# A pinned prologue for an attention and GLU kernel: one written order for four engines

## The chip, the cores and the metric

One core of a Trainium2 chip. The core's engines run side by side, each with an instruction stream of its own: TensorE (PE, matrix products), VectorE (DVE), ScalarE (ACT), GpSimd (POOL) and SyncE (SP, which issues the DMAs here). Matrix products land in PSUM, eight banks of 128 x 512 fp32; all else lives in SBUF. The metric is the device time of one launch in microseconds, the median of several runs.

## The reference

One transformer block with adaptive layer norm, on 2048 rows of 512: attention with 32 query heads of width 16 that share one key and one value head, then a gated feed-forward network of width 1792. Cut to what matters:

```python
mod = (silu(c) @ w_mod).reshape(1, 6, 1, 512)
sa, ca, ga, sb, cb, gb = (mod[:, i] for i in range(6))
h = layernorm(x) * (1 + ca) + sa
q, k, v = h @ wq, h @ wk, h @ wv          # q in 32 heads of 16; k and v one head of 16
p = softmax(q k^T * 16 ** -0.5)           # over 2048 keys
x = x + ga * ((p v) @ wo)
h = layernorm(x) * (1 + cb) + sb
out = x + gb * ((sigmoid(h @ w_gate) * (h @ w_up)) @ w_down)
```

Inputs and outputs are fp32. Most products run in fp16 with each operand split into a high and a low half, so that one product of full precision is three products (`passes`).

## The kernel before

The 2048 rows are four blocks of 512 (`b`). The kernel has three parts.

**Prologue.** Per block: the statistics and the normalization of layer norm (`row_norm`, line 253, called by `ln1_norm`), transposes to put the 512 features on partitions (`ln1_tr`, four chunks `k`), the evacuation that applies scale and shift and splits into high and low fp16 (`ln1_ev` with `split_evac`, line 276: high on ACT, the full fp32 part on ACT or DVE, and the difference on POOL or DVE), and the key and value products (`kv_block`, which writes the keys `kp`). The modulation vectors come from `mod_part`, `mod_cols` and `mod_rows`: four narrow fp32 products (`pmod`), a copy on ACT (`mod`), a product that sums the four parts (`pcol` or `prow`), and a last copy. Two query groups (a group is 128 query columns, four pairs of heads, of one block) are made here; each goes to DRAM (`qD`) and comes back in another layout (`qp`, `load_q`).

Before a score can be exponentiated its row's maximum over all keys is needed. So each *unit* (512 queries of four heads; 32 units in all, eight per block) has 64 score products `sa` with a maximum on DVE each (`a_tile`), then `max_end` and `max_rows`, which put the maxima as extra rows into `qp`, where the second score product `st` subtracts them. The prologue ends with the first `A0 = 76` of these maxima. In unit 0 they go query tile by query tile, so that a first tile's rows (`max_rows`) are ready early; `parts` then gives unit 0's `st` and `c` products as quarters of 128 columns that follow the query tiles.

The prologue's steps stand in the order of a short `PLAN`, but nothing is pinned there: `Ordered` keeps the order of PE, DVE and ACT only when `pinned` is filled, which happens at its end. Until then a scheduler reorders all engines by its own model. All banks of PSUM but one are one pool (`bank`); `cbank` is the accumulator.

**Main loop.** 32 units of 16 steps, PE, DVE and ACT in the written order. Each step has four `st` products with an exponential each (ACT), four `sa` products with a maximum each (DVE) for the units ahead, and the product with the values into `c` (`pv`, two steps behind). In block 0 the query groups that the prologue did not make run beside the steps, two groups as a couple over 17 steps (`light`, `early`); from block 1 on the feed-forward network of the block before does. At the end of a unit `unit_end` copies the accumulator (`cs`, DVE) and starts the next unit's. POOL splits the weights (`weight_jobs`).

**Tail.** The feed-forward network of the last block, not pinned.

Nearly all instructions of PE, DVE and ACT in the main loop are recorded at line 116, that of `Ordered`, so they are told apart by their tiles.

Of the kernel before, what the change touches and what calls it, by code (L numbers as in the profile page):

```python
# [16 lines left out]
P = 128  # L17
S = 2048
D = 512
H = 32  # L20
# [15 lines left out]
PLAN = 'n1 x2 l0 k0 x3 t1 l3 e1 w0 l1 n2 w3 k1 w1 q00 n3 q01 t2 t3 e2 e3 l2 m a1 k2 a2 k3 a4 w2 a8 p z3 a12 z4 a16 z2 a18 z5'  # L36

E32 = [(0, 1), (1, 1), (2, 0), (3, 3), (3, 1)]
ELO = [(0, 3), (0, 1), (3, 1), (3, 2), (2, 1), (3, 0), (1, 1)]

# [26 lines left out]
def adaln_mqa_glu_kernel(  # L67
# [24 lines left out]
    pc = ctx.enter_context(tc.tile_pool(name="pc", bufs=1, space=PSUM))  # L92
    psum = {}
    psum["ctx"] = ExitStack()
    psum["b"] = psum["ctx"].enter_context(tc.tile_pool(name="ps", bufs=1, space=PSUM))
# [4 lines left out]
    def bank(name):  # L100
        return psum["b"].tile([P, 512], F32, tag="b", name=name, bufs=psum.get("n", 7))

    def sbank(name):
        return psum["s"].tile([P, 512], F32, tag=name, name=name, bufs=SBANKS[name]) if "s" in psum else bank(name)

    def cbank(name):
        return pc.tile([P, 512], F32, tag="c", name=name, bufs=1)
# [10 lines left out]
    pinned = []  # L118
    pe, dve, act = Ordered(nc.tensor), Ordered(nc.vector), Ordered(nc.scalar)

# [78 lines left out]
    load_x(0)  # L199
    load_mod(1)  # L200
    load_mod(0)
# [17 lines left out]
    def mod_part(i):  # L219
        p_ = bank("pmod")  # L220
        for k in range(NDC):
            pe.matmul(p_[32 * k:32 * (k + 1)], cbc[:, k, :], wmods[i][:, k, :], start=True, stop=True)  # L222
        t_ = t32("mod")
        act.activation(t_, p_, AF.Identity)
        return t_

    def mod_cols(i, mul, add, name, t_=None):
        res = cp.tile([P, NDC], F32, name=name)
        t_ = mod_part(i) if t_ is None else t_
        p_ = bank("pcol")  # L230
        for m in range(NDC):
            pe.matmul(p_[:, m:m + 1], t_[:, m * P:(m + 1) * P], sel[:, 0:1], start=True, stop=True)
        dve.tensor_scalar(res, p_[:, :NDC], add, mul, op0=ALU.add, op1=ALU.mult)
        return res

    def mod_rows(i, scale, name):
        g_ = cp.tile([P, D], F32, name=name)
        t_ = mod_part(i)
        p_ = bank("prow")
        pe.matmul(p_, sel, t_, start=True, stop=True)  # L240
        act.activation(g_, p_, AF.Identity, scale=scale)
        return g_
# [33 lines left out]
    def split_evac(src, k, sc, sh, hi, lo, e32=None, elo=None):  # L276
        h32 = t32("h32")
        if pinned:
            act.activation(h32, src, AF.Identity, scale=sc[:, k:k + 1], bias=sh[:, k:k + 1])
            pool.tensor_scalar(hi, h32, 1.0, 0.0, op0=ALU.mult, op1=ALU.add)  # L280
            pool.tensor_tensor(lo, h32, hi, op=ALU.subtract)
            return
        act.activation(hi, src, AF.Identity, scale=sc[:, k:k + 1], bias=sh[:, k:k + 1])  # L283
        if e32 is None:
            act.activation(h32, src, AF.Identity, scale=sc[:, k:k + 1], bias=sh[:, k:k + 1])
        else:
            e32.tensor_scalar(h32, src, sc[:, k:k + 1], sh[:, k:k + 1], op0=ALU.mult, op1=ALU.add)
        (elo or pool).tensor_tensor(lo, h32, hi, op=ALU.subtract)


    kbias = cp.tile([P, 1], F32, name="kbias")
    pool.memset(kbias, 0.0)
    for j in (32, 96):
        pool.memset(kbias[j:j + 32], -SM)
        pool.memset(kbias[j:j + 16], 0.0)
# [6 lines left out]
    for t_, s_ in zip(wkr, (wkvh, wkvl)):  # L302
        dve.memset(t_, 0.0)
        for j in (0, 16, 32, 64, 80, 96):
            dve.tensor_copy(t_[:, :, j:j + DH], s_[:, 0])
# [9 lines left out]
    def split_wq(o):  # L315
        cols = slice(o * P, (o + 1) * P)
        w_, hi, lo = wqs.pop(o), wdh[:, :NDC, cols], wdl[:, :NDC, cols]
        act.activation(hi, w_, AF.Identity, scale=SW)
        dve.scalar_tensor_tensor(lo, w_, SW, hi, op0=ALU.mult, op1=ALU.subtract)
# [11 lines left out]
    pts = {}  # L331

    def ln1_norm(b):
        row_norm(xs(b), xs(b))

    def ln1_tr(b, k):
        pts[b, k] = pt = cbank("pt") if k % 4 == 1 else bank("pt")
        for t in range(4):
            pe.transpose(pt[:, t * P:(t + 1) * P], xs(b)[t][:, k * P:(k + 1) * P], ident)

    def ln1_ev(b, k):
        if b not in h1:
            h1[b] = [], []
        hh, hl = h1[b]
        hh.append(t16(f"h1h{k}"))
        hl.append(t16(f"h1l{k}"))
        split_evac(pts.pop((b, k)), k, sc1, sh1, hh[k], hl[k],
                   dve if (b, k) in E32 else None, dve if (b, k) in ELO else None)

    def ln1_block(b):  # L350
        for k in range(NDC):
            if (b, k) not in pts:
                ln1_tr(b, k)
        for k in range(NDC):
            ln1_ev(b, k)
# [4 lines left out]
    def kv_block(b):  # L360
        hh, hl = h1[b]
        pk = bank("pk")
        pv_ = bank("pv")
        n = 0
        for k in range(NDC):
            for w_, h_ in passes(wkr[0], wkr[1], hh[k], hl[k]):
                pe.matmul(pk, w_[:, k, :], h_, start=(n == 0), stop=(n == 3 * NDC - 1))
                n += 1
        for t in range(4):
            n = 0  # L370
            for k in range(NDC):
                for h_, w_ in passes(hh[k], hl[k], wkvh, wkvl):
# [3 lines left out]
        kb = kp[:, b * QB:(b + 1) * QB]  # L376
        act.activation(kb, pk, AF.Identity, scale=1.0 / (SH * SW), bias=kbias)
        for j in (32, 96):
            dve.scalar_tensor_tensor(kb[j:j + DH], pk[j:j + DH, :], 1.0 / (SH * SW), kb[j:j + DH],
                                     op0=ALU.mult, op1=ALU.subtract)  # L380
        dve.tensor_scalar(V[:, b * 4:(b + 1) * 4, 0:DH],
                          pv_[:, :4 * DH].rearrange("p (t d) -> p t d", t=4),
# [4 lines left out]
    def q_group(b, o):  # L387
# [5 lines left out]
        def end(pq, second):  # L393
# [3 lines left out]
            if second:  # L397
                dve.tensor_scalar(q32, pq, 1.0 / (SH * SW), None, op0=ALU.mult)
            else:
                act.activation(q32, pq, AF.Identity, scale=1.0 / (SH * SW))  # L400
            if pinned:
                pool.tensor_scalar(q2[:, 0], q32, 1.0, 0.0, op0=ALU.mult, op1=ALU.add)
            else:
                act.activation(q2[:, 0], pq, AF.Identity, scale=1.0 / (SH * SW))
            pool.tensor_tensor(q2[:, 1], q32, q2[:, 0], op=ALU.subtract)
            sp.dma_start(qD[:, o * P:(o + 1) * P, b * QB:(b + 1) * QB].rearrange("h p q -> p h q"), q2)

        return Group("q", 12, "pq", term, end)

# [11 lines left out]
    def load_q(b, o):  # L421
        qp = wp.tile([P, 4, QB], F16, tag="qp", name="qp", bufs=2)
        for j in (32, 96):
            pool.memset(qp[j:j + 32], 0.0)  # L424
# [18 lines left out]
    def a_tile(i, n):  # L443
        qp, pr0 = get_q(i)
        if i not in mxs:
            mxs[i] = wp.tile([P, 4, 4, 4], F32, tag="mx", name="mx", bufs=2)
        h = n % 4
        kc, qt = (n // 4 % 4, n // 16) if i == 0 else (n // 16, n // 4 % 4)
        j, pr = heads[h]
        sa = sbank("sa")  # L450
        pe.matmul(sa, qp[64 * j:64 * j + 64, pr0 + pr, qt * P:(qt + 1) * P],  # L451
                  kp[64 * j:64 * j + 64, kc * 512:(kc + 1) * 512], start=True, stop=True)
        dve.tensor_reduce(mxs[i][:, 2 * j + pr, qt, kc:kc + 1], sa, axis=AX.X, op=ALU.max)  # L453
        if i == 0 and n % 16 == 15:
            pend.append((i, n // 16, n // 16 + 1))
        elif i > 0 and n == 63:
            pend.append((i, 0, 4))

# [9 lines left out]
    def max_rows(i, t0, t1, m16):  # L468
# [6 lines left out]
        if pinned:  # L475
# [14 lines left out]
    def parts(i, t):  # L490
        if i == 0:
            return [(4 * (t % 4) + n, slice(n * P, (n + 1) * P), slice(t // 4 * P, (t // 4 + 1) * P)) for n in range(4)]
        return [(t, slice(0, QB), slice(0, QB))]

    def st_tile(i, t, pr, j):
# [5 lines left out]
        for kb, cols, qs in parts(i, t):  # L501
            pe.matmul(s_[:, cols], kp[64 * j:64 * j + 64, kb * P:(kb + 1) * P],
                      qp[64 * j:64 * j + 64, pr0 + pr, qs], start=True, stop=True)
# [5 lines left out]
    def pv(i, t, half=None):  # L509
        if t == 0 and half != 1:  # L510
            Cs[i] = cbank("c")
        ps = parts(i, t)
        if half is not None:
            if i == 0:
                ps = ps[2 * half:2 * half + 2]
            else:
                cut = slice(half * QB // 2, (half + 1) * QB // 2)
                ps = [(t, cut, cut)]
        for kb, cols, qs in ps:
            for hh in range(4):  # L520
                pe.matmul(Cs[i][32 * hh:32 * hh + 32, qs], V[:, kb, :], Ps[i, t, hh][:, cols],
                          start=(kb == 0 and (i == 0 or half != 1)), stop=(kb == NKB - 1 and (i == 0 or half != 0)))
# [7 lines left out]
    def unit_end(i):  # L530
# [3 lines left out]
        if pinned:  # L534
# [109 lines left out]
    def ffn_groups(b):  # L644
# [6 lines left out]
        def wo_group(t):  # L651
# [5 lines left out]
            def end(po, second):  # L657
# [3 lines left out]
                if second:  # L661
                    act.activation(t1, po, AF.Identity)
                    pool.tensor_tensor(t1, t1, mods2['ga'], op=ALU.mult)
# [137 lines left out]
    for tok in PLAN.split():  # L801
# [3 lines left out]
        elif f_ == "t":  # L805
            for k in range(NDC):
                ln1_tr(args[0], k)
# [222 lines left out]
```

## Time and profile before

| | |
|---|---|
| median of 3 runs | 1740.53 us (1739.78 to 1742.03) |
| span of the profiled execution | 1738.4 us; the page gives no other time for it |
| busy share of the span | PE 97%, DVE 83%, ACT 71%, POOL 35% |
| the largest groups | exponentials on ACT 1139.2 us, maxima on DVE 1241.2 us |
| prologue, to the first `st` product | 114.9 us |
| block 0, from there to the copy of its eighth unit | to 456.6 us |
| tail, from the last unit's copy | from 1592.4 us |

The page gives busy time per engine, the granted clock of TensorE in 40 slices, the chain of waits that ended last, and groups of instructions with their mean time and the idle time before them. A busy PE is not PE at its peak, since products overlap.

### The profile page before, as it was taken

How to read it: one execution, taken by the hardware profiler on the slowest of the kernel's cores; microseconds unless marked ns; L12 is line 12 of the kernel's file. 1: busy time of each engine (PE TensorE's matmuls, PEld its weight loads, DVE VectorE, ACT ScalarE, POOL GpSimd, SP SyncE). 2: the span in 40 equal slices, each digit the busy share in tenths (PEclk: the TensorE clock that was granted, in tenths of full speed). 3: DMA queues.
4: the chain of work that ended last, by engine and by line, in shares of the span. 5: the costliest groups of instructions: out<-in, count | busy, mean ns of one | idle time of the engine just before them, and what ended most of it. 6: DMA issues, size and time to landing. Idle time of an engine off the chain costs nothing.

```text
span 1738.4 us, 35892 instructions
## 1 busy us (share of the span) xinstructions
PE 1691.9 (97%) x14467; PEld 591.1 (34%) x14467; DVE 1443.2 (83%) x2407; ACT 1226.3 (71%) x2231; POOL 605.1 (35%) x715
## 2 busy tenths in 40 slices
PE   5889999999999999999999999999999999999998
PEld 3335333333233333333333333333333333333443
DVE  8889999999998988888899898988898888841311
ACT  3338888888878777777778777777778777774100
POOL 4131445454443332332245232233255141231433
PEclk9769999999999999999999999999999999999999
DMA  7111223231100110111111110011101010011211
GB/s 262 40 47 31 95 85 106 89 110 63 51 23 26 47 49 12 33 38 41 32 41 33 33 50 20 26 47 47 36 17 57 28 57 5 30 50 55 75 60 49
DMA packets 66238, 90.94 MB, mean 52 GB/s; under 512 B 14752, under 2 KB 41376, under 8 KB 66072
## 3 DMA queue, kind: packets, MB, share of 16 engines
q1 hardware_dynamic: 66072, 88.66, 15.6%
q8 instruction: 113, 1.85, 0.4%
q14 instruction: 53, 0.43, 0.1%
HBM read 67.68 MB, written 16.22 MB: 48 GB/s over the span
## 4 chain that ended last, share of the span: by engine, by line
PE 86%; DVE 7%; ACT 2%; POOL 1%; issue 1%; DMA 1%; SPq 0%; POOLq 0%; DVEq 0%; ACTq 0%
PE c L116 27%; PE st L116 20%; PE pgu L116 12%; PE sa L116 8%; PE pd L116 5%; PE pgu L139 4%; DVE mx L116 3%; PE pd L139 2%; PE pq L116 2%; PE po L116 2%; ACT P L116 2%; PE sa L451 1%; DVE mx L453 1%; PE pmod L222 1%; PE pt L116 1%
## 5 line engine op out<-in xcount | busy, mean ns | idle before, releaser
L116 ACT ACTIVATE P<-st 128x512 f32<-128x512 f32 x2048 | 1139.2, 595 | 283.7 <-PE sa L116 250.0
L116 DVE TENSOR_REDUCE mx<-sa 128x1 f32<-128x512 f32 x1972 | 1241.2, 684 | 113.6 <-PE sa L116 108.3
L116 PE MATMUL st<-qp,kp 64*128 64x512 f16 (+1 forms) x2240 | 746.8, 362 | 7.1 <-DVE mx L453 2.4
L116 PE MATMUL sa<-kp,qp 64*128 64x512 f16 x1972 | 725.3, 382 | 0.5 <-DVE mx L116 0.5
L116 PE MATMUL c<-P,V 128*32 128x512 f32 (+2 forms) x5552 | 577.6, 492 | 2.9 <-DVE cs L116 2.9
L116 PEld LDWEIGHTS <-kp 64*128 64x128 f16 x2240 | 187.8, 94 | 500.1 <-issue 407.2
L116 PE MATMUL pgu<-h2h,gw 64*128 64x512 f16 x1344 | 242.6, 376 | 0.0
L116 PEld LDWEIGHTS <-qp 64*128 64x128 f16 x1972 | 181.8, 93 | 137.0 <-issue 51.9
L116 PEld LDWEIGHTS c<-P,V 128*32 128x32 f32 x5552 | 111.5, 108 | 192.1 <-issue 177.3
L727 POOL TENSOR_SCALAR th<-th 128x512 f32<-128x512 f32 x42 | 26.0, 619 | 335.8 <-ACT th L116 325.8
L116 PE MATMUL pgu<-h2l,gw 64*128 64x512 f16 x672 | 132.3, 376 | 0.0
L116 PEld LDWEIGHTS <-gw 64*128 64x128 f16 x2016 | 99.6, 94 | 80.7 <-issue 3.1
L424 POOL MEMSET qp<- 32x2048 f16 x32 | 57.6, 1798 | 49.3 <-PE st L116 41.6
L139 PE MATMUL pgu<-h2h,gw 128*128 128x512 f16 x224 | 66.8, 379 | 0.5 <-ACT h2h L283 0.5
L733 POOL TENSOR_TENSOR gl<-th,gh 128x512 f16<-128x512 f32 x56 | 64.8, 1157 | 4.7
L478 POOL TENSOR_SCALAR mh<-m 16x128 f16<-16x128 f32 (+1 forms) x34 | 9.8, 288 | 159.3 <-ACT m L116 159.0
L730 DVE SCALAR_TENSOR_TENSOR th<-th,pgu 128x512 f32<-128x512 f32 x14 | 9.6, 688 | 66.3 <-PE pgu L139 53.0
L248 POOL TENSOR_SCALAR wst<-wst 128x512 f32<-128x512 f32 x46 | 28.5, 620 | 102.1 <-DMA wst<-in_B_w_down_dram 27.1
L721 ACT ACTIVATE th<-pgu 128x512 f32<-128x512 f32 x14 | 8.4, 597 | 76.9 <-PE pgu L139 76.9
L116 DVE COPY u<-pgu 128x512 f32<-128x512 f32 x42 | 28.5, 679 | 35.7 <-PE st L116 19.8
L750 POOL TENSOR_TENSOR ot<-ot,gb 128x512 f32<-128x512 f32 x10 | 12.7, 1273 | 126.7 <-ACT ot L116 126.7
L590 POOL TENSOR_TENSOR raw<-raw,rb 128x512 f32<-128x512 f32 x15 | 19.1, 1273 | 102.7 <-DMA rb<-lD 84.1
(164 smaller groups left out, 1435.3 us busy)
## 6 DMA issues: line engine op xcount, KB each, us to landing
gw<-wD SPq DMA_DIRECT2D x56, 512.0 KB
wD<-gw SPq DMA_DIRECT2D x14, 512.0 KB
wm<-in_w_mod_dram SPq DMA_DIRECT2D x6, 1024.0 KB
qp<-qD SPq DMA_DIRECT2D x96, 64.0 KB
xall<-in_A_x_dram SPq DMA_DIRECT2D x4, 1024.0 KB
qD<-q SPq DMA_DIRECT2D x16, 256.0 KB
raw<-cs SPq DMA_DIRECT2D x128, 32.0 KB
xr<-in_A_x_dram SPq DMA_DIRECT2D x16, 256.0 KB
```

Of the source, the lines that this page charges most:

```text
L116: return (lambda *a, **k: keep(f_(*a, **k))) if pinned else f_
L139: pe.matmul(self.bank, l_, r_, start=(n == 0), stop=(n == self.n - 1))
L222: pe.matmul(p_[32 * k:32 * (k + 1)], cbc[:, k, :], wmods[i][:, k, :], start=True, stop=True)
L248: pool.tensor_scalar(w_, w_, SW, 0.0, op0=ALU.mult, op1=ALU.add)
L424: pool.memset(qp[j:j + 32], 0.0)
L451: pe.matmul(sa, qp[64 * j:64 * j + 64, pr0 + pr, qt * P:(qt + 1) * P], kp[64 * j:64 * j + 64, kc * 512:(kc + 1) * 512], start=True, stop=True)
L453: dve.tensor_reduce(mxs[i][:, 2 * j + pr, qt, kc:kc + 1], sa, axis=AX.X, op=ALU.max)
L478: pool.tensor_scalar(mh[:, 0], m32, 1.0, 0.0, op0=ALU.mult, op1=ALU.add)
L590: keep(pool.tensor_tensor(raw, raw, rb, op=ALU.mult))
L727: pool.tensor_scalar(th, th, 1.0, 1.0, op0=ALU.add, op1=ALU.mult)
L733: pool.tensor_tensor(lo, th, hi, op=ALU.subtract)
L750: pool.tensor_tensor(ot, ot, mods2['gb'], op=ALU.mult)
```

## The change

1. `PLAN` becomes a list of some 400 tokens, one per small stage. Each names one operation on one engine (`S` statistics of a tile, `ra`/`rb`/`rc` the inverse root, `N` normalization, `T` transposes, `H` high half, `E` full part, `L` low half, `pk`/`KB`/`KL` keys, `pv`/`V` values, `q`/`QA`/`QL` a query group, `pm`/`me`/`pr`/`m` modulation, `a` a score product, `x` its maximum, `mx` the row maxima of one query tile, `wh`/`wl` the split of query weights, `lw`/`lx`/`lm` loads, `bl` the clearing of a `qp`). `pinned` is filled from the start, so PE, DVE and ACT keep the list's order, and POOL too through `pool1`.
2. Places: block 0 is normalized on DVE, blocks 1 to 3 on POOL (`NORM`); nearly all low halves are made on POOL and the full parts on ACT (`H32`, `HLO`); three of four low halves of the query weights on POOL.
3. Unit 0's 64 maxima go quarter of the keys by quarter of the keys, as in the other units, so `parts` is gone and unit 0's products have 512 columns. All four of its row maxima are made in the prologue.
4. Six query groups in the prologue in place of two; five couples in block 0 in place of seven.
5. Keys: one high copy on ACT with a scale per partition and one pass on DVE over 128 partitions, in place of one and two of 16. The copies of key weights into `wkr` move to ACT (four in place of twelve).
6. In block 0 `cs` is copied on ACT; a couple's second query copy is on ACT too.
7. The first modulation part is loaded ahead of x, whose first block comes in four loads. PSUM in the prologue is four banks for `bank` and four for `sa`.
8. `split_evac` keeps only its second form (full part on ACT, high and low on POOL), which the tail now uses too.

```diff
-PLAN = 'n1 x2 l0 k0 x3 t1 l3 e1 w0 l1 n2 w3 k1 w1 q00 n3 q01 t2 t3 e2 e3 l2 m a1 k2 a2 k3 a4 w2 a8 p z3 a12 z4 a16 z2 a18 z5'
+PLAN = (
+    'lw0 lx2 lx3 lw1 lw2 lw3 lm4 lm3 lm2 lm5 pm1 S00 S01 me1 S02 pr1 S03 ra0 rb0 m1 rc0 pm0 N00 N01 N02 N03 me0 T00 '
+    'S10 pr0 wh0 S11 S12 wl0 T01 m0 S13 H00 T02 E01 E00 T03 ra1 H01 S20 L00 H02 E03 E02 L01 rb1 q000 H03 S21 pk00 '
+    'L02 wh1 rc1 q001 L03 pk01 N10 wh2 S22 q002 N11 S23 wh3 q003 ra2 N12 S30 pk02 rb2 QA00 S31 pk03 S32 pv0 N13 KB0 '
+    'rc2 S33 QL00 T10 KL0 N20 ra3 T11 V0 H10 rb3 T12 E10 T13 H11 L10 rc3 E11 H12 pm4 L11 E12 H13 pk10 N21 E13 pk11 '
+    'L12 me4 a a a L13 x pk12 x a a pr4 x N22 x N23 pk13 m4 x a N30 T20 KB1 x N31 T21 KL1 H20 N32 T22 E20 N33 T23 '
+    'H21 E21 L20 a a a x a H22 x a T30 L21 E22 x H23 a x a pk20 L22 E23 x pk21 x H30 a L23 x pk22 E30 x a a a x L30 '
+    'pk23 x a a KB2 T31 x wl1 x pk30 H31 KL2 a wl2 a E31 a x T32 x a L31 T33 H32 x E32 x a a wl3 pk31 x H33 a x a '
+    'E33 pv1 L32 x x a a x L33 bl pk32 x a a x pv2 x x pk33 V1 V2 a a KB3 x a a pm3 x KL3 a a me3 x pm2 x a pr3 x '
...
+NORM = ('DDDD', 'PPPP', 'PPPP', 'PPPP')
+H32 = ('ADAD', 'AAAA', 'AAAA', 'AAAA')
+HLO = ('PDPD', 'PPPP', 'PPPP', 'PPPP')
...
-    pinned = []
+    pinned, first = [True], [True]
     pe, dve, act = Ordered(nc.tensor), Ordered(nc.vector), Ordered(nc.scalar)
+    pool1 = Ordered(nc.gpsimd)
...
-        if pinned:
-            act.activation(h32, src, AF.Identity, scale=sc[:, k:k + 1], bias=sh[:, k:k + 1])
-            pool.tensor_scalar(hi, h32, 1.0, 0.0, op0=ALU.mult, op1=ALU.add)
-            pool.tensor_tensor(lo, h32, hi, op=ALU.subtract)
-            return
-        act.activation(hi, src, AF.Identity, scale=sc[:, k:k + 1], bias=sh[:, k:k + 1])
...
+        act.activation(h32, src, AF.Identity, scale=sc[:, k:k + 1], bias=sh[:, k:k + 1])
+        pool.tensor_scalar(hi, h32, 1.0, 0.0, op0=ALU.mult, op1=ALU.add)
+        pool.tensor_tensor(lo, h32, hi, op=ALU.subtract)
...
+    def ln_norm(b, t):
+        mv, ve, rs, nw = lns[b]
+        eng = dve if NORM[b][t] == 'D' else pool1
+        eng.tensor_scalar(xs(b)[t], xs(b)[t], mv[:, t, 0:1], rs[:, t:t + 1], op0=ALU.subtract, op1=ALU.mult)
...
+    def ln1_low(b, k):
+        eng = dve if HLO[b][k] == 'D' else pool1
+        eng.tensor_tensor(h1[b][1][k], h32s.pop((b, k)), h1[b][0][k], op=ALU.subtract)
...
+    def k_high(b):
+        pks[b, "h"] = kh = t16("kh")
+        act.activation(kh, pks[b], AF.Identity, scale=kscale, bias=kbias)
+
+    def k_end(b):
+        dve.scalar_tensor_tensor(kp[:, b * QB:(b + 1) * QB], pks[b], 1.0 / (SH * SW), pks.pop((b, "h")),
+                                 op0=ALU.mult, op1=ALU.subtract)
...
-            if second:
-                dve.tensor_scalar(q32, pq, 1.0 / (SH * SW), None, op0=ALU.mult)
-            else:
-                act.activation(q32, pq, AF.Identity, scale=1.0 / (SH * SW))
...
+            act.activation(q32, pq, AF.Identity, scale=1.0 / (SH * SW))
+            if first:
                 act.activation(q2[:, 0], pq, AF.Identity, scale=1.0 / (SH * SW))
+                q2s[b, o] = q2, q32
+                return
...
-        kc, qt = (n // 4 % 4, n // 16) if i == 0 else (n // 16, n // 4 % 4)
+        kc, qt = n // 16, n // 4 % 4
...
-    def parts(i, t):
-        if i == 0:
-            return [(4 * (t % 4) + n, slice(n * P, (n + 1) * P), slice(t // 4 * P, (t // 4 + 1) * P)) for n in range(4)]
-        return [(t, slice(0, QB), slice(0, QB))]
...
-        if pinned:
+        if pinned and b > 0:
             dve.tensor_copy(cs, Cs.pop(i))
         else:
             act.activation(cs, Cs.pop(i), AF.Identity)
...
     for tok in PLAN.split():
...
+        name = tok.rstrip("0123456789")
+        stages[name](*[int(z) for z in tok[len(name):]])
+    assert not held and apos == A0
+    first.clear()
...
-    pinned.append(True)
```

The rest of the list holds the remaining scores and maxima, the modulation parts 3, 2 and 5, the last value products, the four `mx`, and the query groups q01 to q03, q10 and q11, product by product between the scores.

More of the change, by code (lines that the diff above doesn't have):

```diff
@@ L198, in adaln_mqa_glu_kernel @@
     sp.dma_start(wkv[:, 1], wv.rearrange("(k p) n -> p k n", p=P))
-    load_x(0)
     load_mod(1)
+    for t in range(4):
+        sp.dma_start(xall[:, t, :], x[t * P:(t + 1) * P, :])
     load_mod(0)
@@ L771, in adaln_mqa_glu_kernel, with a_next @@
     apos = 0
[L773 removed]
+    held = []
+    def a_next():
         nonlocal apos
[L775 to L799 removed]
```

309 lines of the change are left out of this document (151 added, 158 removed), and 4 rows, old and new, of the table PLAN.

## The prediction

> **What bounds the kernel now.** I read the page first, then busy time by stretches, then the chain of waits, then the groups of the stretches that the change touches.
>
> ```profile
> span 1738.4 us, 35892 instructions
> ...
> PEclk9769999999999999999999999999999999999999
> ```
> The profiled execution spans 1738.4 us; the median of the runs is 1740.5, so 2.1 us lie around the span. Each slice is 43.5 us: only in the first three is the clock of TensorE (PE) low.
>
> ```profile
> core 0: us, PE busy (x) PEld busy (x) DVE busy (x) ACT busy (x) POOL busy (x), PEclk, DMA share, GB/s
> 43.00:51.50 8.50, 7.69 (x83) 5.27 (x80) 4.04 (x6) 5.41 (x10) 3.48 (x3) 1.00 0.24 79
> 74.00:84.00 10.00, 8.67 (x27) 2.80 (x27) 8.78 (x17) 0.60 (x1) 0.00 (x0) 0.50 0.00 0
> 51.10:114.90 63.80, 52.42 (x254) 16.73 (x256) 55.82 (x97) 11.99 (x19) 13.28 (x17) 0.65 0.13 40
> 164.30:205.90 41.60, 41.35 (x435) 13.11 (x429) 40.74 (x68) 36.18 (x67) 21.92 (x26) 1.00 0.32 103
> 432.45:456.60 24.15, 23.49 (x233) 7.05 (x230) 23.93 (x42) 21.07 (x41) 12.35 (x14) 1.00 0.15 47
> ```
> Columns are length, busy time of each engine, granted clock. The prologue's second part (51.1 to 114.9) is paced by VectorE (DVE), 55.8 of 63.8, at a clock of 0.65. Two units of block 0 follow: the whole unit 1 (164.3 to 205.9) with an early query couple beside it, and the end of the block (432.45 to 456.6) without one.
>
> ```profile
> L453 DVE TENSOR_REDUCE mx<-sa 128x1 f32<-128x512 f32 x76 | 46.7, 681 | 8.1 <-PE sa L451 8.0
> 95.61 9.66 DVE L453 TENSOR_REDUCE mx<-sa 128x1 f32<-128x512 f32 x16 [0.38 <-PE sa L451]
> 44.69 2.42 DMA qD<-q
> 51.10 0.69 DVE L453 TENSOR_REDUCE mx<-sa 128x1 f32<-128x512 f32 x1 [3.37 <-PE sa L451]
> 114.86 0.21 PE L116 MATMUL st<-qp,kp 64*128 64x128 f16 x1 [2.35 <-DVE mx L453]
> ```
> The groups of DVE, its timeline and the chain: 76 maxima at 9.66/16 = 0.604 us, the first 6.4 us after the first queries leave for DRAM (44.69 to 51.10), the last just before the main loop starts at 114.9. Nothing before 44.69 is a maximum, so the prologue is a chain of about 45 us and then 46 us of maxima that are padded to 64.
>
> **The prologue: when the maxima start.** The new list keeps 76 maxima and pins four engines in its order. So a late operation holds all that stands behind it on its engine. The operation to look at is the normalization: 12 of 16 go from DVE to GpSimd (POOL).
>
> ```profile
> L274 DVE TENSOR_SCALAR xall<-xall,mv,rs x16: 509/542/1376, 13.0 to 35.3; 128x512 f32<-128x512 f32 x16
> L274 POOL TENSOR_SCALAR t<-xr,mv,rs x12: 2085/2096/2099, 498.5 to 1287.8; 128x512 f32<-128x512 f32 x12
> L280 POOL TENSOR_SCALAR h2h<-h x12: 618/620/623, 530.1 to 1314.3; 128x512 f16<-128x512 f32 x12
> L288 POOL TENSOR_TENSOR h1l<-h,h1h x9: 1152/1160/1380, 23.7 to 65.8; 128x512 f16<-128x512 f32 x9
> 11.38 1.03 POOL L263 TENSOR_TENSOR rs<-ve,mhalf 128x4 f32<-128x4 f32 x1 [0.80 <-DVE ve L262]
> ```
> The main loop already runs this very operation on POOL, at 2.10 us against 0.54 on DVE; POOL's operation with constants in place of the two per-row scalars takes 0.62. I take 2.10, as form and line are the same.
>
> The Trainium skill's "GPSIMD Engine Reference" (section 4.1, Engine selection) calls one-input elementwise work on GpSimd roughly line-rate; the 2.10 beside 0.54 speaks against that here, and what the rule would give is the first rival.
>
> ```profile
> 15.91 2.47 DVE L259 BATCH_NORM_STATS2 st<-xall 128x6 f32<-128x512 f32 x4 [0.96 <-DMA xall<-in_A_x_dram]
> 79.24 1.98 PE pmod L222 x8
> 81.30 0.61 ACT mod L224
> 81.95 1.87 PE pcol L232 x8
> 23.49 1.45 ACT L283 ACTIVATE h1h<-pt,sa,ca 128x512 f16<-128x512 f32 x2
> GB/s 0 0 37 63 301 383 272 397 389 408 408 412 361 408 406 414 406 412 406 410 410 410 408 395 410 406 410 408 410 408 369 345 252 21 16 0 0 0 0 0
> ```
> The last row is what the loads moved in each of the first 40 us: 11.4 MB by 34, in either order. Start: x's second block is the fourth large load in both orders, so it lands at 15.9 again. On DVE the last modulation column (m0) then stands behind three statistics of 0.62 and one wl0 (0.7): 18.8, with pm0, me0 and pr0 (1.98 + 0.61 + 1.87 after a landing one megabyte, 2.6 us at 405 GB/s, earlier: 17.8) done by then. H00 and E00 (1.45 for two) give 20.2. On POOL follow L00 (1.16), rb1 (1.03) and L02 (1.16): the first normalization of block 1, N10, starts at about 23.6.
>
> From N10 to L23, the last operand of block 2's keys, POOL runs in order 12 normalizations (25.2), 8 subtractions (9.3), two powers (2.1) and QL00 (1.2): 37.8 us, to 61.4. In it, QL00 stands behind N13: four normalizations and rb2 after 23.6 put its end at 34.2, so by the 6.4 us above the first maximum comes at 40.6, 10.5 earlier than before. Then TensorE waits in order at T20 for N23 and at T30 for N33, and scores stand behind both: by the list only 18 maxima lie ahead of KL2, 11 us of work in the 23 from 40.6. pk23, KB2 and KL2 add about 0.7 each (below, and 0.69 for a DVE pass):
>
> ```profile
> 53.51 1.62 PE pk L367 x7
> 39.97 2.35 PE pq L139 x10
> 18.01 3.09 PE pt L339 x14
> 83.82 1.90 PE sa L451 x8
> 85.73 0.58 PE sa L451
> 104.39 2.08 PE prow L240 x2
> L379 DVE SCALAR_TENSOR_TENSOR kp<-pk,kp x8: 682/690/698, 35.9 to 69.1; 16x512 f16<-16x512 f32 x8
> ```
> KL2 ends at 63.5.
>
> **From there to the main loop.** DVE still has 58 maxima (35.0), KL3 (0.7), and some 3.6 for V, m3 and the four row maxima (an estimate: three V copies, one column, four times three small passes, at 0.2 to 0.3 each as I read them in the groups): 39.3, so not before 102.8. PE has 57 score products at 0.24 (1.90/8, back to back), 13.6; 20 query parts of three products at 0.235, 14.1; nine key products, 2.1; eight transposes, 1.8; three modulation products, 5.9; one column sum and two row sums, 6.0: 43.5, and three V products besides, for which I add nothing since the fp32 prices here are those of a clock of 0.50. So PE paces this stretch, not DVE: 43.5 to 107.0, and I allow 0.5 for the hand-off. The main loop starts at **107.5**, 7.4 us earlier. Bounds: 102.8 (DVE alone), and 112 (8.1 us of DVE idling as in the row of the 76 maxima, on top of 39.3, is 110.9, with a us for the V products).
>
> The four moved query groups are in the 43.5 (twelve more parts, 8.5 us). What else moves is covered: ScalarE, which takes the key copies, second weight halves and query copies, was busy 12.0 of 63.8; the loads that wait for a slot (lm2, lm5) wait on SP for pm1 and pm0, and the first writer behind them, qD, comes at 34.2, after the loads. All four row maxima now go out ahead of the loop:
>
> ```profile
> 116.89 3.86 SPq L487 DMA_DIRECT2D qp<-mh  x6
> ```
> SP spends 0.64 on each of four issues per quarter; the last quarter's stand 12 maxima (7.2) before the loop, which covers 2.6 and the 2.4 of a landing like qD's. Without that cover the loop's first score would wait those 5.
>
> **Block 0.**
>
> ```profile
> 164.31 0.68 DVE L116 COPY cs<-c 128x512 f32<-128x512 f32 x1
> 431.86 0.68 DVE L116 TENSOR_SCALAR q<-pq 128x512 f32<-128x512 f32 x1
> 456.57 0.68 DVE L116 COPY cs<-c 128x512 f32<-128x512 f32 x1
> 432.79 0.37 PE L116 MATMUL st<-qp,kp 64*128 64x512 f16 x1 [0.16 <-ACT P L116]
> ```
> From 114.9 to the eighth unit's copy at 456.6 lie 130 steps, 341.7 us. Seven couples (14 groups, 17 steps each) become five: 85 steps keep the pace with a couple, 41.6/16 = 2.60, or 221.0. The other 45 run as the end of the block does: 24.15 for 39 maxima, 2.48 a step, or 111.5. Sum 332.5, so 9.2 less; 2.5 of that is the stumbling start of unit 0 (49.4 for 18 steps against 46.8), which waits for three query tiles' rows and runs quarters of tiles. The copies of C to ScalarE free DVE of 0.6 per unit, worth 1.8 in the three units that DVE paces, and nothing where PE does. Both query copies now follow each other on ScalarE: the one there already made a score wait 0.16; I charge 0.5 per couple, 2.5. A cold clock at the hand-off keeps about 1 of the 2.5. Sum: 9.2 + 1.8 - 2.5 - 1.0 = **7.5 less**; bounds 3 (only the 34 freed steps, 34 x 0.12 = 4.1, less 1) and 11.
>
> **The tail.** The branch that made high and full parts side by side on ScalarE is gone; the last block now takes the full part, then high and low on POOL.
>
> ```profile
> 1622.97 0.77 ACT L285 ACTIVATE h<-pt,sh,sc 128x512 f32<-128x512 f32 x1
> 1623.12 0.38 PE L139 MATMUL pgu<-h2h,gw 128*128 128x512 f16 x1 [0.54 <-ACT h2h L283]
> 1627.84 1.16 POOL L288 TENSOR_TENSOR h2l<-h,h2h 128x512 f16<-128x512 f32 x1 [0.18 <-ACT h L285]
> ```
> POOL needs 4 x (0.62 + 1.16) = 7.1 after the first full part at 1623.0, so the last low part comes at 1630.1 instead of 1629.0, the first high one at 1623.6 instead of 1623.0. PE is the bound there: I add **1.0**, between 0.6 and 2.5.
>
> **Sum.** 1738.4 - 7.4 - 7.5 + 1.0 = 1724.5, and with 2.1 around it 1726.6 us.
>
> **The rivals.**
>
> Fast normalization on POOL: at 0.62, POOL's 37.8 becomes 20.0 and QL00 ends at 28.3; its write queues behind the last loads, so the first maximum comes at 35 to 38. From there DVE has 76 maxima and about 6 more, 52, with 5 of idling: the main loop at 92 to 95, 20 to 23 earlier, and the time 1711 to 1714. For it speaks only that the copied buffer differs from the main loop's; the 12 rows within 14 ns speak against.
>
> Cold PE, the slower side: in 74 to 84 PE was busy 8.67 of 10 and yet granted 0.50. After waiting for N23 and N33 it may enter the stretch from 63.5 cold and stay so. Query, key and transpose work doubles (14.1 + 2.1 + 1.8 more), and half of the scores come singly at 0.58 (9.7 more): 43.5 becomes 71, the main loop starts at 134.7, and the time is 1740.5 + 19.8 - 7.5 + 1.0 = 1754. It decides once that stretch takes over 57.9 us. Against it: with full-height query products, 43 to 51.5, the clock was 1.00.
>
> The Trainium skill's "TensorE: Matmul & The Clock Gate" (Part 1, The HAM clock gate) has the clock released after some 3.4 us of sustained work; by that rule the sum stays. The row of 74 to 84 does not agree if busy time is what is meant.
>
> Block 0 gives nothing: if ScalarE's added copies hold up scores as much as the couples free, only the prologue's 7.4 less 1.0 is left: 1734.
>
> **How the numbers follow.** A measurement of this kernel tells about 0.2%, 3.5 us, from no change. Forecast 0.57, its own range 1718 to 1735; fast POOL 0.13; block 0 gives nothing 0.15; cold PE 0.15. Faster: 0.55 + 0.13 + 0.13 = 0.81; same 0.04; slower 0.15. The range from 1711 to 1738 leaves out the cold case and little else.
>
> **What would show it.** Right: POOL's xall normalization at 2.1 us and POOL busy without a gap from 24 to 61; T20 and T30 released by POOL; first maximum near 40.6, main loop near 107.5; steps of 2.60 up to the fifth couple, then 2.48; the tail's first gate product held by POOL. Wrong: a normalization under 1 us, a granted clock near 0.5 beyond 70 us, a first maximum beyond 45, or block 0's steps unchanged after the fifth couple.

## The result, and the profile after

| | before | after | forecast |
|---|---|---|---|
| time, median of four runs each | 1740.82 us (1739.78 to 1742.03) | 1729.68 us (1729.02 to 1730.17) | 1726.6 us |
| span of the profiled execution | 1738.4 | 1727.5 | 1724.5 |
| first `st` product (end of the prologue) | 114.86 | 108.72 (-6.1) | 107.5 (-7.4) |
| block 0, from there to the eighth `cs` | 341.7 | 337.1 (-4.6) | -7.5 |
| eighth `cs` to the last one (blocks 1 to 3) | 1135.85 | 1136.32 (+0.5) | 0 |
| tail, last `cs` to the end of the span | 146.0 | 145.4 (-0.6) | +1.0 |

The ratio of the times is 0.9935, interval 0.9921 to 0.9949: 11 us less, inside the range. The prologue and block 0 gave it, as forecast, each by less than forecast; the tail did not cost.

The page of the changed kernel, its span and the granted clock:

```profile
span 1727.5 us, 34861 instructions
...
PEclk9899999999999999999999999999999999999999
```
The clock of the third slice is no longer low. The stretches of the changed kernel, with the columns of before (length, busy time of each engine, granted clock, DMA):

```profile
40.00:63.50 23.50, 17.69 (x69) 7.59 (x67) 12.46 (x21) 8.60 (x14) 23.50 (x16) 0.78 0.03 10
63.50:80.00 16.50, 16.38 (x179) 7.45 (x177) 16.11 (x31) 7.40 (x11) 9.66 (x8) 1.00 0.00 1
80.00:100.00 20.00, 18.91 (x123) 6.01 (x116) 16.92 (x35) 3.92 (x8) 2.31 (x2) 1.00 0.11 38
155.85:197.97 42.12, 41.15 (x435) 13.07 (x432) 40.00 (x66) 36.98 (x69) 21.89 (x26) 1.00 0.31 102
365.06:406.07 41.01, 39.44 (x387) 11.76 (x385) 39.78 (x67) 35.48 (x68) 17.77 (x23) 1.00 0.15 48
406.07:445.80 39.73, 39.33 (x387) 11.73 (x385) 39.54 (x66) 35.44 (x68) 13.73 (x16) 1.00 0.15 44
```
From 40 to 63.5 POOL is busy in all of the 23.5 us: it is the engine that paces there, and no longer DVE (12.46). From 63.5 to 100 PE has 35.29 of 36.5, at clock 1.00. The last three rows are a unit of block 0 with a couple beside it, one in which the couples are over, and the last.

POOL's timeline holds the chain, and those of PE and DVE what hangs on it:

```profile
24.59 6.57 POOL L129 TENSOR_SCALAR xall<-xall,mv,rs 128x512 f32<-128x512 f32 x3 [0.52 <-DVE rs L129]
34.20 1.15 POOL L129 TENSOR_TENSOR q<-q,q 128x512 f16<-128x512 f32 x1
44.93 12.35 POOL L129 TENSOR_SCALAR xall<-xall,mv,rs 128x512 f32<-128x512 f32 x6
57.24 5.60 POOL L129 TENSOR_TENSOR h1l<-h,h1h 128x512 f16<-128x512 f32 x5
```
```profile
41.65 0.69 DVE L129 TENSOR_REDUCE mx<-sa 128x1 f32<-128x512 f32 x1
55.28 0.33 PE L129 MATMUL pt<-ident,xall 128*128 128x128 f32 x1 [1.66 <-POOL xall L129]
64.75 0.68 DVE L129 SCALAR_TENSOR_TENSOR kp<-pk,kh 128x512 f16<-128x512 f32 x1
108.72 0.39 PE L129 MATMUL st<-qp,kp 64*128 64x512 f16 x1
```
A normalization on POOL takes 12.35/6 = 2.06 us. N10 starts the chain at 24.59, QL00 (the `q` row) ends at 35.35, the first maximum follows at 41.65, PE's transpose at 55.28 waited for a normalization, KL2 (the third block's `kp`, which starts at 64.75 and ends at 65.43) closes the chain, and 44.0 us after its start the main loop starts at 108.72, now with a product of 512 columns.

Block 0 and the tail, by the copies of C (`cs`: units 0, 1, 7 and the last of all) and the tail's first gate products, from the timelines of ACT, DVE, POOL and PE:

```profile
155.85 0.60 ACT L129 ACTIVATE cs<-c 128x512 f32<-128x512 f32 x1
197.97 0.60 ACT L129 ACTIVATE cs<-c 128x512 f32<-128x512 f32 x1
445.80 0.60 ACT L129 ACTIVATE cs<-c 128x512 f32<-128x512 f32 x1
1582.12 0.69 DVE L129 COPY cs<-c 128x512 f32<-128x512 f32 x1 [3.30 <-PE c L129]
```
```profile
1612.86 0.62 POOL L304 TENSOR_SCALAR h2h<-h 128x512 f16<-128x512 f32 x1
1613.53 1.46 PE L153 MATMUL pgu<-h2h,gw 128*128 128x512 f16 x6 [1.25 <-POOL h2h L304]
1614.82 0.38 PE L153 MATMUL pgu<-h2l,gw 128*128 128x512 f16 x1
```

### The profile page after: what moved, and what is told of

Same layout as the page of the kernel before. It is cut to its first block, busy times and chain, and to the rows that moved or that the text cites. A ratio compares the mean times of both kernels' runs of the same rounds, so it can differ in the third digit from the quotient of the medians.

```text
span 1727.5 us, 34861 instructions
## 1 busy us (share of the span) xinstructions
PE 1685.0 (98%) x13971; PEld 571.6 (33%) x13971; DVE 1422.0 (82%) x2359; ACT 1236.0 (72%) x2253; POOL 635.2 (37%) x732
## 4 chain that ended last, share of the span: by engine, by line
PE 89%; DVE 4%; POOL 3%; ACT 2%; DMA 1%; issue 1%; SPq 0%; POOLq 0%; DVEq 0%; ACTq 0%
PE c L129 29%; PE st L129 22%; PE pgu L129 12%; PE sa L129 9%; PE pd L129 5%; PE pgu L153 4%; PE pq L129 2%; PE pd L153 2%; DVE mx L129 2%; PE po L129 2%; ACT P L129 2%; POOL xall L129 1%; DMA xall<-in_A_x_dram 1%; PE pt L129 1%; PE po L153 1%
## 5 line engine op out<-in xcount | busy, mean ns | idle before, releaser
L129 DVE TENSOR_REDUCE mx<-sa 128x1 f32<-128x512 f32 x2048 | 1289.3, 683 | 126.3 <-PE sa L129 120.5
L129 PE MATMUL st<-qp,kp 64*128 64x512 f16 x2048 | 747.0, 379 | 8.9 <-ACT P L129 4.6
L129 PE MATMUL sa<-kp,qp 64*128 64x512 f16 x2048 | 747.8, 383 | 3.4 <-DVE mh L129 1.5
L129 PE MATMUL c<-P,V 128*32 128x512 f32 (+1 forms) x5296 | 577.1, 508 | 0.7 <-ACT cs L129 0.4
L129 PEld LDWEIGHTS <-kp 64*128 64x128 f16 x2048 | 174.1, 94 | 497.3 <-issue 409.3
L129 PEld LDWEIGHTS <-qp 64*128 64x128 f16 x2048 | 186.7, 93 | 175.9 <-issue 93.1
L129 PEld LDWEIGHTS c<-P,V 128*32 128x32 f32 x5296 | 104.4, 108 | 189.1 <-issue 179.8
L492 POOL MEMSET qp<- 32x2048 f16 x28 | 50.3, 1798 | 48.6 <-PE st L129 36.9
L555 POOL TENSOR_SCALAR mh<-m 16x128 f16<-16x128 f32 x31 | 8.9, 288 | 139.0 <-ACT m L129 138.6
```

The lines of the kernel that those rows point to most:

```text
L129: return (lambda *a, **k: keep(f_(*a, **k))) if pinned else f_
L492: eng.memset(qp[j:j + 32], 0.0)
L555: pool.tensor_scalar(mh[:, 0], m32, 1.0, 0.0, op0=ALU.mult, op1=ALU.add)
```

## The experiments

The theory is that of the prediction: POOL's normalizations pace the prologue up to KL2, PE paces it from there, and block 0 gains by the couples that are gone. Each kernel is the changed one with the edit shown. All ratios are against the kernel before, measured again beside each experiment. Where two kernels differ by less than the 3.5 us that a measurement tells apart, I go by the positions in their traces and say so. Four of the traces below have the same prologue to the letter (the changed kernel, and those with another query copy, another `cs` and another tail): KL2 starts in them at 64.75, 66.08, 65.72 and 64.68, so a position there can move by 1.4 us without any edit.

**All normalizations on DVE, or three blocks on ACT.** Without POOL's 12 times 2.1 us.

```diff
-NORM = ('DDDD', 'PPPP', 'PPPP', 'PPPP')
+NORM = ('DDDD', 'DDDD', 'DDDD', 'DDDD')
```


> The changed kernel, with all 16 normalizations on VectorE. Theory (GpSimd's 2.1 us normalizations pace the prologue up to 64.8 us): GpSimd loses 25 us of work ahead of the second block's low halves, the first maximum comes at 35 to 37 instead of 41.7 (then held by the last loads), TensorE no longer waits at T20 and T30, VectorE takes 12 x 0.5 = 6 us more, and the first st product comes at 95 to 99 instead of 108.7; time 1717 to 1721. Rival (TensorE's own sum and the written order pace the prologue whoever normalizes): the first st product within 3 us of 108.7; time 1727 to 1730.

```diff
+NORM = ('DDDD', 'AAAA', 'AAAA', 'AAAA')
...
+        dve.scalar_tensor_tensor(nb, mv[:, :, 0], -1.0, rs, op0=ALU.mult, op1=ALU.mult)
...
+        if NORM[b][t] == 'A':
+            act.activation(xs(b)[t], xs(b)[t], AF.Identity, scale=rs[:, t:t + 1], bias=nb[:, t:t + 1])
+            return
```


> The changed kernel, with the 12 normalizations of blocks 1 to 3 on ScalarE (scale and a bias of minus mean times scale, one small VectorE pass per block more). Theory: as with VectorE, but VectorE keeps its 6 us, and ScalarE, idle for half of the prologue, takes 12 x 0.6; the four of block 1 stand ahead of the first query copy there and delay it by 2 to 3 us, which the last loads hide. First st product at 92 to 97; time 1714 to 1719. Rival (TensorE paces whoever normalizes): within 3 us of 108.7; time 1727 to 1730.

DVE: 1724.29 us, ratio 0.9896 (0.9881 to 0.9911). ACT: 1723.81 us, 0.9896 (0.9881 to 0.991). Spans 1722.5 both, first `st` product at 104.2 both. The chain of waits and DVE's timeline of the first, then of the second:

```profile
30.49 7.57 DMA qD<-q
41.78 0.69 DVE L129 TENSOR_REDUCE mx<-sa 128x1 f32<-128x512 f32 x1 [2.24 <-PE sa L129]
60.24 0.68 DVE L129 SCALAR_TENSOR_TENSOR kp<-pk,kh 128x512 f16<-128x512 f32 x1
```
```profile
31.83 6.35 DMA qD<-q
42.11 0.69 DVE L129 TENSOR_REDUCE mx<-sa 128x1 f32<-128x512 f32 x1 [6.66 <-PE sa L129]
```
The main loop comes 4.5 us earlier, so POOL's normalizations do cost the change that much. But the first maximum did not move (41.78 and 42.11 beside 41.65): the queries were ready 4.9 and 3.5 us earlier, and their write to DRAM then took 7.57 and 6.35 us. In the changed kernel it goes out at 35.38, when the loads are through, and the read-back follows at 37.72. What moved the main loop is KL2, 4.5 earlier. Both theories' numbers missed: mine gave a larger gain, the rival less than 3 us.

**That write, with the loads behind it.** With the normalizations on ACT, the loads of three modulation parts (3 MB, first used at 74 us in the changed kernel) go behind the first score; SyncE's order is written out so that they stay there.

```diff
-    'lw0 lx2 lx3 lw1 lw2 lw3 lm4 lm3 lm2 lm5 pm1 S00 ...
+    'lw0 lx2 lx3 lw1 lw2 lw3 lm4 pm1 S00 ...
-    ... me4 a a a L13 ...
+    ... me4 a lm3 lm2 lm5 a a L13 ...
+    sp1 = Ordered(nc.sync)
```


> Normalizations on ScalarE as in the run before, and the modulation loads 3, 2 and 5 (3 MB) issued behind the first queries' write and read-back, in an order kept on SyncE. There the write was issued at 31.8 and took 6.4 us, against 2.4 in the kernel before. Theory (it queues behind those loads): it takes 2.4 again, the first maximum comes at 37 to 38 instead of 42.1, the second block's keys at 56 to 57 instead of 60.3 and the first st product at 99 to 101 instead of 104.2; time 1719 to 1721. Rival (something else on TensorE paces 42 to 60): the maximum comes earlier, the st product stays within 1 us of 104.2; time 1723 to 1724.

1718.30 us, 0.9868 (0.9853 to 0.9882), 5.5 us under the same kernel with the loads in their old place. The chain, and the group of `st` products (its row has the first and last start):

```profile
31.81 2.31 DMA qD<-q
L133 PE MATMUL st<-qp,kp x2048: 372/376/388, 98.1 to 1568.4; 64*128 64x512 f16 x187
```
The same write, issued at the same time, takes 2.31 us; the first maximum is at 37.8, KL2 at 54.16, the main loop at 98.1. So once POOL is out of the way it is the queue of loads that holds the first queries, and most of the gain that I had expected of the two kernels above comes only with both. SyncE's written order came with the late loads and has no run of its own.

**The written order itself.** The list stays, but nothing is pinned until the prologue's end: the scheduler orders it.

```diff
-    pinned, first = [True], [True]
+    pinned, first = [], [True]
...
     first.clear()
+    pinned.append(True)
```


> The changed kernel, with the prologue's four engines not pinned: the same stages, places and list, but the scheduler orders them. In its order GpSimd does the eight normalizations of blocks 1 and 2 before the first query's low half. Theory (order on GpSimd sets the first maximum): four normalizations more stand ahead of it, the first maximum comes 6 to 9 us later than 41.7, and the end follows by part of it: first st product at 110 to 118; time 1731 to 1739. Rival (places and stages make the gain, and the scheduler does as well or better): first st product at 105 to 109; time 1726 to 1730.

The same, with normalizations on ACT:

> The unpinned kernel with the normalizations of blocks 1 to 3 on ScalarE (pinned, this was 1723.8 with the first st product at 104.2; unpinned with GpSimd's, 1748.0 and 126.1). Theory (the written order is worth 17 us only because it spreads GpSimd's slow normalizations, which the scheduler puts ahead of the first query's low half): the first maximum comes at 42 to 45 instead of 55.9, the st product at 104 to 110; time 1724 to 1730. Rival (the order is worth as much whoever normalizes): st product 17 us later than pinned, at 119 to 123; time 1739 to 1743.

Unpinned: 1747.99 us, 1.0034 (1.0022 to 1.0046), slower than before; first `st` product at 126.1, later than I expected. POOL's and DVE's timelines:

```profile
31.02 8.26 POOL L389 TENSOR_SCALAR xall<-xall,mv,rs 128x512 f32<-128x512 f32 x4
...
40.28 8.24 POOL L389 TENSOR_SCALAR xall<-xall,mv,rs 128x512 f32<-128x512 f32 x4
48.49 1.15 POOL L473 TENSOR_TENSOR q<-q,q 128x512 f16<-128x512 f32 x1
55.94 0.69 DVE L529 TENSOR_REDUCE mx<-sa 128x1 f32<-128x512 f32 x1 [8.03 <-PE sa L522]
```
Two blocks' normalizations now stand ahead of the first queries' low half, which ends at 49.6 in place of 35.35.

Unpinned with ACT: 1731.64 us, 0.9944 (0.9926 to 0.9963), main loop at 110.2 where the pinned one with ACT has 104.2; both numbers are just past the edge of what I expected. DVE still waits for scores, 18.4 us in 17 waits of up to 4.5, by the waits from 44 to 112 us:

```profile
DVE mx L533 <- PE sa L526: 18.4, 17, 4.5
```
So in these kernels the order is worth 6.0 us of prologue when no engine has slow work, and 17.4 with POOL's normalizations (126.1 to 108.7). Without the list those normalizations cost 15.9 (126.1 beside 110.2) and not 4.5, and the kernel with them is slower than the one before.

**Six groups, or two, in the prologue.** The tokens of `q02`, `q03`, `q10` and `q11` are taken out, so block 0 has seven couples again.

> The changed kernel with two query groups in the prologue and seven couples in block 0, as before. Theory (TensorE paces the prologue from 64.8 on): 16 query parts at about 1.07 us go, VectorE's 39 us then set the end at 104 to 105.5 instead of 108.7, and 34 steps of block 0 cost 42.1/16 - 39.7/16 = 0.15 more each, 5.1; time 1729 to 1732, so moving the four groups was worth 0 to 2 us. Rival (the moved groups were hidden in the prologue, since VectorE paces it): the st product stays at 108 to 109, and the time is 1734 to 1735.

1731.53 us, 0.9944 (0.9927 to 0.996); by the trace the main loop starts at 105.9, 2.8 us earlier, and block 0 takes 342.9, 5.8 more: the four groups are worth 3.0 by these marks, 2.7 by the spans (1730.2), and 2.1 if the later KL2 (65.65) is put down to chance. The times, 1.9 apart, do not tell it from nothing. One stretch of its prologue and its `st` group:

```profile
100.00:110.00 10.00, 8.51 (x21) 1.74 (x21) 9.75 (x18) 2.08 (x4) 5.99 (x8) 0.50 0.22 60
L132 PE MATMUL st<-qp,kp x2048: 372/376/631, 105.9 to 1581.9; 64*128 64x512 f16 x187
```
Without the query products at the end only half-height products are left (scores, and from 105.9 on the first `st`), and the clock is 0.50 as in before's 74 to 84. It fell while PE waited for DVE: PE is busy for 1.04 of the 2.5 us from 90 to 92.5, and the clock is 0.56 in the next 2.5. It then stayed at 0.50 from 100 to 106, where PE is busy for 5.72 of 6. The sixteen query parts that the prologue is spared cost 0.75 each in the chain of the changed kernel, 12.0 together, and give back 3.7 of the stretch behind KL2, since DVE sets the pace there (9.75 of 10).

**Scores in twos.** In the changed kernel's chain of waits the scores between query products stand single:

```profile
84.26 0.75 PE pq L129 x3
85.01 0.32 PE sa L129
85.33 0.75 PE pq L129 x3
```
A lone score costs 0.32, not the 0.24 that I took from eight back to back; two together cost 0.32 as well, for example at 86.08 in the same chain. Here the last scores are put two at a time between the query parts, the maxima as they were.

```diff
-    'a q010 x a q011 x a x a q012 x a x q013 ...
+    'a q010 x a a q011 x x a a q012 x x q013 ...
```


> The changed kernel, with the last 26 or so score products of the list put in twos instead of singly between the query parts (the maxima's order unchanged). Theory (TensorE paces there, and two scores on the two halves of the rows run together): about ten times 0.2 to 0.3 us less, the first st product at 106 to 107; time 2 to 3 us less than 1729.7. Rival (the row maxima, for which VectorE waits 0.9 four times, or VectorE itself pace it): no change.

1727.63 us, 0.9922 (0.9907 to 0.9936). The time alone cannot tell it from 1729.68; by the trace the main loop starts at 107.3, although KL2 came 0.4 later (65.15), so the stretch behind KL2 is 1.8 shorter:

```profile
L133 PE MATMUL st<-qp,kp x2048: 372/376/388, 107.3 to 1577.6; 64*128 64x512 f16 x187
```

From the start of KL2 to the main loop, in the kernels that keep the pinned list:

| kernel | KL2 | first `st` | between |
|---|---|---|---|
| changed | 64.75 | 108.72 | 44.0 |
| norm. on DVE | 60.24 | 104.2 | 44.0 |
| norm. on ACT | 60.28 | 104.2 | 43.9 |
| ACT, late loads | 54.16 | 98.1 | 43.9 |
| query copy on DVE (below) | 66.08 | 110.0 | 43.9 |
| `cs` on DVE (below) | 65.72 | 109.7 | 44.0 |
| tail as it was (below) | 64.68 | 108.7 | 44.0 |
| scores in twos | 65.15 | 107.3 | 42.2 |
| two groups | 65.65 | 105.9 | 40.3 |
| all that helped (below) | 53.05 | 95.2 | 42.2 |

In the first seven rows KL2 moves by 11.9 us and the stretch behind it by 0.1; only what changes PE's work in it changes it. So that stretch has a price of its own, whatever happens ahead of it.

**The copies in block 0.** The couple's second query copy back on DVE, then `cs` back on DVE:

```diff
+            if second:
+                dve.tensor_scalar(q32, pq, 1.0 / (SH * SW), None, op0=ALU.mult)
+            else:
+                act.activation(q32, pq, AF.Identity, scale=1.0 / (SH * SW))
```


> The changed kernel, with a couple's second query copy back on VectorE. Units 1 to 4 of block 0 took 41.95 to 42.13 us against 41.6 to 41.8 before. Theory (two query copies in a row on ScalarE hold the next scores): those units fall back to 41.6 to 41.8, 0.4 less each for five couples; time about 2 us less, 1727.7. Rival (the copy of C on ScalarE costs it): no change, units stay at 42.1.

```diff
-        if pinned and b > 0:
+        if pinned:
```


> The changed kernel, with the copy of C in block 0 back on VectorE. Theory (this copy is worth nothing where TensorE paces and 0.6 us per unit where VectorE does): units 1 to 4 within 0.1 of 42.1 us, unit 7 0.6 longer than 39.7; time 0 to 2 us more. Rival (it is what costs 0.4 in units 1 to 4): these fall to 41.7; time 2 us less.

Query copy on DVE: 1727.87 us, 0.992 (0.9905 to 0.9935). Its `cs` on ACT, at the ends of units 1 and 2:

```profile
197.97 0.60 ACT L129 ACTIVATE cs<-c 128x512 f32<-128x512 f32 x1
239.64 0.60 ACT L129 ACTIVATE cs<-c 128x512 f32<-128x512 f32 x1
```
The coupled units 2 to 4 take 41.67, 41.47, 41.67 in place of 42.13, 41.95, 42.13: 0.46 less each, and the second copy on ACT costs what was charged. But block 0 as a whole takes 336.8 in this trace beside 337.1: unit 6 took 43.9 in place of 41.0, with PE waiting there for 2.6 us in place of 0.9 for row maxima that come back from DRAM. So the gain shows in the units and not in this trace's span (1728.1). In the kernel of all that helped (below), which has the same edit, that wait is 0.9 again.

`cs` on DVE: 1730.35 us, 0.9932 (0.9915 to 0.9949). The coupled unit 1 is 0.36 shorter than in the changed kernel (41.76), units 2 to 4 are 0.14 to 0.16 longer. The three last units take 122.5 together in place of 121.6: the last has 40.07 in place of 39.73, and unit 6, with 41.50 in place of 41.01, again waits longer for row maxima (1.3 in place of 0.9). So `cs` on ACT is worth 0.4 to 0.9 in all, at most half of the 1.8 that I counted. Both edits are too small for the times and are read from the traces.

**The tail as it was.**

```diff
+        if tail:
+            act.activation(hi, src, AF.Identity, scale=sc[:, k:k + 1], bias=sh[:, k:k + 1])
+            act.activation(h32, src, AF.Identity, scale=sc[:, k:k + 1], bias=sh[:, k:k + 1])
+            pool.tensor_tensor(lo, h32, hi, op=ALU.subtract)
+            return
```


> The changed kernel, with the tail's evacuation as before (high and full part on ScalarE, the low one on GpSimd). From the last unit's copy to the end of the span the kernel before took 145.9 us and the changed one 145.4. Theory (PE has enough high-half products to do while the later low halves come, so the new form costs nothing): 145.2 to 146.0; time within 1 us of 1729.7. Rival (the form costs what the prediction charged): 144.4 or less; time 1 us less or more.

1730.70 us, 0.9936 (0.9919 to 0.9953); last `cs` at 1582.17, so a tail of 145.7 beside 145.4. PE in it:

```profile
1612.88 1.04 PE L153 MATMUL pgu<-h2h,gw 128*128 128x512 f16 x4 [0.54 <-ACT h2h L304]
1614.78 0.38 PE L153 MATMUL pgu<-h2l,gw 128*128 128x512 f16 x1 [0.85 <-POOL h2l L306]
```
With the old form the first product starts 0.65 earlier, and PE then waits 0.85 for the low part. With the new form it starts later and runs six products through to the low part: 1614.82 beside 1614.78. The chain through the low part sets the place, and that did not move. The tails differ by 0.3, which one trace each cannot settle.

**All that helped, together:** normalizations on ACT, late loads, the second query copy on DVE, scores in twos.

> Normalizations on ScalarE, the three modulation loads late, a couple's second query copy on VectorE, and the scores in twos. Theory: the gains add, since each lies in another stretch: first st product at 96 to 99, coupled units of 41.6; time 1714 to 1718. Rival (one of them uncovers the next bound, VectorE's own 39 us from the second block's keys on): first st product at 100 or later; time 1719 to 1722.

1714.54 us, 0.9849 (0.9834 to 0.9864), faster than both kernels: 15 us below the change, 27 below before.

```profile
L133 PE MATMUL st<-qp,kp x2048: 372/376/631, 95.2 to 1564.2; 64*128 64x512 f16 x187
```
First maximum 37.5, KL2 53.05, then 42.2 as with scores in twos; block 0 takes 335.5, with 41.1 for unit 6.

Points 3, 5 and 7 of the change (the order of unit 0's maxima, the keys, the first loads and the banks) have no run that takes back one of them alone; what each is worth stays open.

## Why the prediction was right, and where not

**The prologue, forecast -7.4, measured -6.1.** The chain was the right one: normalization at 2.06 to 2.19 us (forecast 2.10), POOL busy without a gap, T30's transposes held by POOL (T20, also named, did not wait). N10 came at 24.59 and not 23.6; the 0.52 that it waited for the inverse root on DVE is half of that, and where the other half arose among the operations ahead of it I did not follow. L23 then ended at 61.7, only 0.3 later than forecast. The term that was too small is the next one, pk23, KB2 and KL2 at about 0.7 each: KL2 ended at 65.4 and not 63.5, 3.7 behind L23 and not 2.1. PE had scores and key products left over behind T30, which the last normalization held to 57.3, and worked them off at a granted clock of 0.51 from 57.5 to 60 and 0.87 from 60 to 63.5; on DVE four maxima stood ahead of KL2:

```profile
62.35 2.48 DVE L129 TENSOR_REDUCE mx<-sa 128x1 f32<-128x512 f32 x4 [0.38 <-PE sa L129]
```
The main loop is 1.2 us later than forecast, less than the 1.4 by which KL2 moves between traces of the same prologue.

From the end of KL2 the forecast had 44.0 to the main loop, and it was 43.3. That this came so close is partly luck. The pace was PE's, as the two stretches and the table of KL2 show, but the terms of the sum were off both ways. In the chain of waits behind KL2 the three modulation products and the three sums take 6.1 and not 11.9, for they were priced from rows at a clock of 0.50 and ran at 1.00. The V products, for which nothing was added, take 3.9, and the row maxima, which were not in the sum, take 2.3 on DVE between the scores. The scores take 12.2 for 13.6 and the query parts 15.0 for 14.1. The four moved groups, finally, are sixteen query parts and not twelve; the sum itself held all twenty of its stretch.

**Block 0, forecast -7.5, measured -4.6.** The first 82 steps (unit 0 and the four coupled units) went better than the sum: by 2.60 a step, 0.5 a couple and 1.0 of cold clock 216.6, measured 215.5 (108.72 to 324.18). The 0.5 was confirmed as 0.46. The step that failed is the rate of the free ones: the last three units were to take 7.8 for three coupled steps, 111.6 for 45 free ones, less 1.8 for `cs`, plus 0.1: 117.7; they took 121.6. I had read 2.48 from an undisturbed end of a block, 24.15 for 39 maxima, and the last unit does run at it, but only with `cs` on ACT (39.73/16 = 2.48, beside 2.50 with it on DVE); that copy gave at most 0.9 and not 1.8. Unit 6 took 41.01, and PE waits there once, for 0.9, for row maxima that come back from DRAM:

```profile
PE st L129 <- DMA qp<-mh: 0.9, 1, 0.9
```
That unit is 1.3 over the last one, which has no such wait, and I had priced it at nothing; with the query copy on DVE the wait is 2.6 and the unit 4.2 over the last one. Unit 5, with the last three coupled steps, took 40.88, 1.4 over the forecast for it. With the second query copy on DVE it took 40.39, so that copy is 0.5 of it; the cause of the rest stays open.

The kernel before could have told this. By the same rates its block 0 is 119 steps of 2.60, 11 of 2.48 and the 2.5 of unit 0, 339.2 us, and it took 341.7; its unit 6 has 42.65 beside 41.83 for unit 5. So 2.5 of the 9.2 that I took off are what the rates leave out in the kernel before already, and no gain of the change. Without them the sum gives 5.0 less, beside the measured 4.6.

**The tail, forecast +1.0, measured -0.6.** Wrong in sign. The high part did come later, as forecast (the product starts 31.4 us after the last `cs`, before 30.7), but I charged a later start of PE as a later end. PE had a wait for the low part behind it, which took up the delay. The last low part ended 38.1 us after the last `cs` in place of 36.6, and PE did not wait for it: low parts at 0.62 + 1.16 each did not become the bound. The remaining 0.6 is within what I can read from one trace.

**The rivals.** Fast POOL fell by its condition: 2.06 us. Its numbers were wrong too: it let the first maximum come at 35 to 38, while with early queries the write waited 7.57 us behind loads and the maximum came at 41.8, and with normalizations off POOL the main loop came at 104.2; its 92 to 95 was only nearly reached (95.2) when two other obstacles, the loads and the lone scores, were taken away as well. The Trainium skill's "GPSIMD Engine Reference" (section 4.1, Engine selection), which calls one-input work there roughly line-rate, would have had it otherwise; with two per-row scalars, no run here shows line rate on POOL.

Cold PE fell: PE did leave its wait for N33 at a clock of 0.51, but was granted 1.00 from 63.5 to 100. The kernel with two groups shows that the mechanism exists, 0.50 from 100 to 110 when only half-height products are left. It lacks the mixed-in query products, full in height, that the case against this rival named; whether their height or their number keeps the clock up, no run separates. The rule in the Trainium skill's "TensorE: Matmul & The Clock Gate" (Part 1, The HAM clock gate), some 3.4 us of sustained work for the full clock, agrees with the 1.00 and not with that row, where PE is busy 8.51 of 10, if busy time is what is meant.

That block 0 gives nothing fell by -4.6, and the slower side was reached only by the unpinned list.

## What to carry to other kernels

When work moves to a slower engine under a written order, add up that engine's whole list to the last operand that another engine waits for: here some 37 us on POOL, not DVE's or PE's load, set the first 62 us, and the sum of the list ended within 0.3 of the trace. Before counting on an earlier result, look at what its transfer queues behind: with queries 4 us earlier the first maximum did not move until 3 MB of loads that nobody needed yet stood behind them. A rate taken from the undisturbed end of a stage is a lower bound for the stage. Put such rates on the kernel before first and compare with its measured time: what they miss there is no gain of the change.

## What was not expected of the hardware

- A write of the same size took 7.57 or 6.35 us when loads stood ahead of it in its issuer's order and 2.31 when they stood behind it.
- One half-height score between full-height products cost 0.32 us in the chain; putting the last ones in twos took 1.8 us from a stretch of 44.
- TensorE, busy 8.5 of 10 us with half-height products alone, was granted 0.50, and 1.00 for 36 us with full-height products among them.
- Between traces of the same prologue a step at 65 us moved by up to 1.4 us (64.68 to 66.08).
